# A fused attention and MLP kernel: first q load with a cast, k' and q' of the leftover chunks through one exponential, a new instruction order

## The chip, the cores and the metric

The kernel runs on one core of one Trainium2 chip. The metric is the device time of one execution in microseconds (us), as the median of several runs. The profile is that of one execution.

A core has a matmul engine (PE in the profile, its weight loads PEld), a vector engine (DVE), a scalar engine (ACT), GpSimd (POOL) and a queue engine (SP). Each works through its own list of instructions in order and waits on semaphores. Transfers are issued by SP, ACT or POOL and run on 16 shared DMA engines. In this kernel every load that changes the type is issued by POOL.

## The reference

What is computed, with the scale of the attention and the sizes put in:

```python
# q, k, v: (8, 8, 576, 64); omega: (128, 64); w_in: (512, 2048); w_out: (2048, 512)
def phi(x):                                  # x is q or k, times 64 ** -0.25
    h = einsum('bhsd,md->bhsm', x, omega) - (x * x).sum(-1, keepdims=True) / 2
    return exp(h - h.max(-1, keepdims=True)) / sqrt(128)
q_p, k_p = phi(q), phi(k)
kv  = einsum('bhsm,bhsd->bhmd', k_p, v)
num = einsum('bhsm,bhmd->bhsd', q_p, kv)
den = einsum('bhsm,bhm->bhs', q_p, k_p.sum(2)) + 1e-6
x = (num / den) as (8 * 576, 512)            # one row for each token, heads side by side
h = x @ w_in                                 # 4608 x 2048
out = (h * clip(h + 3, 0, 6) / 6) @ w_out    # 4608 x 512
```

## The kernel before

**Tiles.** The kernel goes through the 8 batches. In each batch the 8 heads are four pairs. A head has 576 positions; 512 are the "mains", 64 are the "leftovers". A batch has 36 chunks of 128 rows (`NCH`), held as 18 double chunks (`NDC`): double chunks 0 and 1 hold the leftover rows, 2 to 17 the mains. `TU` cuts the 18 into (0,2), (2,6), (6,10), (10,14), (14,18).

**Attention of a batch.** `load` (L643) brings in k, q and v; the loads of k come as mains `k00` to `k11` and leftovers `kl`, those of q as `q00` to `q11`, `ql0` and `ql1`. In batch 0 k and q arrive as float32 (`k32`, `q32`) through SP and ACT, and PE transposes them as float32 (`turns32`, L742, L748), with an evacuation from PSUM that casts to bfloat16 (the `Tev` operations, L552 on ACT, L553 on DVE). In later batches POOL issues the loads with a cast into `kb` and `qb`; batch 1 is transposed by PE in bfloat16 (`turns`, L756, L564), batches 2 to 7 by a DMA transpose (L803). The projections on omega are matmuls (batch 0: L865 for k, L884 for q; later `burst`, L808, with L822 for k and L825 for q). An exponential on ACT turns a projection in PSUM into k' (`kp`, L872 or L841) or q' (`qpT`, L888 or L849); DVE takes the row maximum of k' (`row_max`, L705). `cc` is its reciprocal; v is scaled with it (`vc` L999/L1001, `vcl` L910, `vcc` L1008/L1009); then come the products with v (`kv`, L1017/L1019), the numerators (`num`, L1045), the division (L1064/L1068) into `xb`, and its transposition into `xT` (batches 2 on: DMA, L1100) and `xS`.

**Leftovers in a burst.** A part of two double chunks, (0,2), gets two PSUM banks. One bank holds the k projection of one half of the double chunks in its first 256 columns and the q projection in its second 256. Before, each half bank has an exponential of its own, and each half of k' a row maximum: four exponentials of 256 columns and two maxima a batch, in batches 1 to 7.

**MLP.** Block b of 512 tokens is worked on while batch b + 1 goes through attention; block 8 holds all the leftover tokens. The first matmul is either plain (`mm1`, L1124: four operations of four 512-column matmuls for a group of four feature tiles) or a scheme of seven products in place of eight (`mm1_quad`, L1199: 28 matmuls of 256 columns at L1222, three PSUM copies, two additions). `FIRST7` gives for each of the four groups the first block that uses the seven products. These need sums of weights (`input_sums`, L1154, L1318) and of tokens (`x_sums`). The second matmul uses such a scheme too (`products`, L1358, L1391). The activation is a relu on ACT (L1130, L1258, L1286) and a product on DVE (L1132, L1260, L1288). Block 0 goes by halves of 256 tokens (`mm1_half`, L1265; half A first), so that it can start before the whole of x is there.

**Opening.** w_in arrives by five loads on POOL (`wi`, L625), gated by `W_GATE` on the landing of `q11`. PE runs matmuls on a constant tile (`idle_work`, L603, L606) where the plan leaves it idle in the first 21 us.

**Order.** Nothing is queued in the order of the code. Every operation has a number, by creation. The table `ORDER` gives for each of the five engines the list of operations in the order in which its queue has them; which engine runs an operation follows from the list it stands in. `schedule` (L209) goes through the lists with a plan of durations (`occ`), of times after an operation's end until others may count on it (`lat`; for batch 0's loads `LANDS`), of issue times and of shared DMA bandwidth (`packet`). From that plan come the PSUM banks, the places of the fillers and the order among engines. Semaphore waits follow from what each operation reads and writes: the kernel computes the same at any plan.

## Time and profile before

| | |
|---|---|
| runs | 299.27, 298.52, 298.09 us; median 298.52 |
| profiled execution | 298.33 us, of which the span from first to last instruction is 296.5 |
| busy: PE, PEld | 289.5 us, 220.1 us |
| busy: DVE, ACT, POOL | 257.4 us, 240.6 us, 182.2 us |
| granted PE clock | 0.999 |
| DMA | 44.90 MB, mean 151 GB/s |

A group's line gives the line of the kernel, the engine, the operation, what it writes and reads, its shape and count, then its busy time and the mean of one (ns), then the idle time of the engine just before such instructions and what ended most of it. A line of the waits gives who waited for whom, the total in us, the number of times and the longest. Matmuls are pipelined and their ends are modelled: a busy PE need not be at its peak. The numbers in `qb`, `kb` and the like are left out of names; several buffers share a name, so `q<-...` at L1318 and L1222 is the former `q32` in its second use, as a store for sums.

### The profile page before, as it was taken

Reading aid. Unit: us, or ns where it says so; the run is one execution under the profiler, and the core shown is the slowest. Engines: PE = TensorE matmul, PEld = TensorE weight load, DVE = VectorE, ACT = ScalarE, POOL = GpSimd, SP = SyncE. Lnnn points to the kernel's source line nnn. Section 1 sums busy time; section 2 is a strip of 40 time slices with the busy share of each in tenths; the row PEclk is TensorE's granted clock in tenths of the full one; section 3 lists DMA queues with packets and bytes.
Section 4 is the critical chain, followed back from the end, with each engine's and each line's share of the span. In section 5 each row is a group of like instructions: output and inputs, shape, how many; then the busy total and the mean of one; then the engine's idle time right before and its main releaser. Section 6 shows DMA issues by size and latency. Waiting matters only on the chain.

```text
span 296.5 us, 7761 instructions
## 1 busy us (share of the span) xinstructions
PE 289.5 (98%) x2938; PEld 220.1 (74%) x2938; DVE 257.4 (87%) x581; ACT 240.6 (81%) x587; POOL 182.2 (61%) x207
## 2 busy tenths in 40 slices
PE   8999999999898999999999999999999999999996
PEld 5768855544784698658856987588787888888885
DVE  4797888869987998899789996999999999998974
ACT  2975988799778998999899887999899988767410
POOL 1666456047697863898798579766667344556241
PEclk9999999999999999999999999999999999999999
DMA  8999999989999997998997999959601500110034
GB/s 234 296 206 196 203 234 117 149 200 229 138 202 207 216 127 207 152 199 234 163 180 130 111 259 168 153 131 234 122 2 35 167 25 0 74 71 2 0 144 142
DMA packets 90100, 44.90 MB, mean 151 GB/s; under 512 B 57936, under 2 KB 87760, under 8 KB 90064
## 3 DMA queue, kind: packets, MB, share of 16 engines
q1 hardware_dynamic: 62496, 31.11, 46.6%
q0 software_dynamic: 26592, 12.46, 33.9%
q10 hardware_dynamic: 976, 0.85, 0.9%
q8 instruction: 23, 0.38, 0.5%
q14 instruction: 13, 0.11, 0.1%
HBM read 36.73 MB, written 9.44 MB: 156 GB/s over the span
## 4 chain that ended last, share of the span: by engine, by line
PE 90%; ACT 6%; DVE 3%; issue 0%
PE p L1391 33%; PE p L1222 20%; PE p L1124 13%; PE p L1302 5%; PE p L1277 5%; PE p L1045 3%; PE p L822 3%; PE p L1017 3%; PE p L825 2%; ACT kp L872 1%; PE p L606 1%; ACT tsb L1130 1%; ACT qpT L849 1%; ACT qpT L888 1%; PE p L564 1%; ACT kp L841 1%
## 5 line engine op out<-in xcount | busy, mean ns | idle before, releaser
L705 DVE TENSOR_REDUCE mx<-kp 128x4 f32<-128x512 bf16 (+1 forms) x79 | 47.8, 629 | 6.1 <-ACT kp L841 4.1
L1258 ACT ACTIVATE tsb<-p 128x512 f16<-128x512 f32 x76 | 44.8, 620 | 8.0 <-DVE gT L1260 4.3
L1260 DVE SCALAR_TENSOR_TENSOR gT<-tsb,p 128x512 f16<-128x512 f16 x76 | 50.0, 679 | 1.4 <-ACT tsb L1258 1.0
L1124 PE MATMUL p<-xT,wi 128*128 128x512 f16 x208 | 49.2, 379 | 1.0 <-ACT qpT L849 0.8
L1391 PE MATMUL p<-wo,gT 128*128 128x256 f16 x368 | 46.2, 273 | 0.8 <-DVE gT L1132 0.8
L552 ACT COPY p<-p 128x512 f32<-128x512 f32 x61 | 35.3, 596 | 7.8 <-PE p L1222 5.8
L841 ACT ACTIVATE kp<-p 128x512 bf16<-128x512 f32 (+1 forms) x70 | 37.3, 578 | 4.8 <-PE p L825 4.8
L1391 PEld LDWEIGHTS p<-wo,gT 128*128 128x128 f16 x368 | 35.2, 98 | 5.3 <-ACT kp L841 1.1
L849 ACT ACTIVATE qpT<-p 128x512 bf16<-128x512 f32 (+1 forms) x70 | 37.7, 577 | 0.8 <-PE p L825 0.7
L1132 DVE SCALAR_TENSOR_TENSOR gT<-tsb,p 128x512 f16<-128x512 f16 x52 | 34.2, 678 | 4.5 <-ACT tsb L1130 4.0
L1124 PEld LDWEIGHTS p<-xT,wi 128*128 128x128 f16 x208 | 19.5, 98 | 22.4 <-ACT qpT L849 1.7
L1130 ACT ACTIVATE tsb<-p 128x512 f16<-128x512 f32 x52 | 31.4, 629 | 3.1 <-PE p L1124 2.7
L999 POOL TENSOR_TENSOR vc<-v,cc 128x512 bf16<-128x512 f32 (+1 forms) x29 | 29.1, 1002 | 7.4 <-DVE s L1318 1.9
L1318 POOL TENSOR_TENSOR gT<-gT 128x512 f16<-128x512 f16 x21 | 24.3, 1156 | 14.1 <-DVE s L1318 10.1
L1391 PE MATMUL p<-t,gT 128*128 128x256 f16 x256 | 31.1, 273 | 0.0
L1318 POOL TENSOR_TENSOR s<-gT,s 128x512 f16<-128x512 f16 x18 | 20.8, 1156 | 13.1 <-DVE s L1318 4.3
L1318 POOL TENSOR_TENSOR gT<-gT,s 128x512 f16<-128x512 f16 x18 | 20.9, 1162 | 12.3 <-PE p L1391 6.7
L1391 PEld LDWEIGHTS p<-t,gT 128*128 128x128 f16 x256 | 24.4, 98 | 5.0 <-issue 1.6
L652 POOL DMA_DIRECT2D kb<-in_k_dram x21 | 16.4, 785 | 18.9 <-DMA kT<-kb 10.9
L1318 POOL TENSOR_TENSOR s<-gT 128x512 f16<-128x512 f16 x15 | 17.4, 1158 | 10.3 <-DVE wi L1318 3.2
L1068 ACT ACTIVATE xb<-p,rec 128x64 f16<-128x64 f32 x98 | 21.9, 365 | 0.5 <-DVE rec L1057 0.5
L652 POOL DMA_DIRECT2D qb<-in_q_dram x28 | 19.7, 708 | 2.9 <-DMA wi<-in_moe_w_in_dram 2.9
(142 smaller groups left out, 640.3 us busy)
## 6 DMA issues: line engine op xcount, KB each, us to landing
v<-in_v_dram SPq DMA_DIRECT2D x14, 512.0 KB, 4.7
out_dram<-osb SPq DMA_DIRECT2D x14, 512.0 KB, 3.8
kb<-in_k_dram POOLq DMA_DIRECT2D x14, 256.0 KB, 6.2
qb<-in_q_dram POOLq DMA_DIRECT2D x14, 256.0 KB, 6.2
wo<-in_moe_w_out_dram POOLq DMA_DIRECT2D x8, 256.0 KB, 6.7
wi<-in_moe_w_in_dram POOLq DMA_DIRECT2D x3, 512.0 KB, 7.5
q<-in_q_dram SPq DMA_DIRECT2D x4, 256.0 KB, 4.5
vl<-in_v_dram SPq DMA_DIRECT2D x8, 128.0 KB, 3.8
```

What stands on the lines that cost most here:

```text
L552: return E.copy(dst(), src())
L652: lambda E: E.dma_start(dst, src), prio + 0.001 * turn_of[0], reads=gate, writes=keys,
L705: op("DVE", dvet(128 * n), lambda E: E.reduce_max(dst, src, axis=AX.X), p, reads=reads, writes=writes, name="mx" + name)
L841: op("ACT", actt(128 * (d1 - d0)), lambda E, lh=lh, ko=ko, part=part: E.activation(ko, out_of(part, 0, lh)[0].rearrange("p (x m) -> p x m" ...
L849: op("ACT", actt(128 * (d1 - d0)), lambda E, lh=lh, part=part: E.activation(qd[:, part[0]:part[1], lh, :], out_of(part, 1, lh)[0].rearrang ...
L1124: ins = E.matmul(ring.t[vh.slot], wi[:, c, 128 * f:128 * f + 128], xv[:, c, :], start=(c == 0), stop=(c == NJ - 1))
L1130: op("ACT", actt(512), lambda E: E.activation(tsb[tu][:], ring.t[vh.slot], AF.Relu, bias=0.5, scale=1.0 / 6.0), t - 0.1, reads=[vh], write ...
L1222: ins = E.matmul(bank(v)[:, 256 * g:256 * g + 256], w(c, f + g), x[:, c, :], start=start and g == 0 and c == 0, stop=c == 1, skip_group_ch ...
L1258: op("ACT", actt(512), lambda E, v=v, tu=tu: E.activation(tsb[tu][:], bank(v), AF.Relu, bias=0.5, scale=1.0 / 6.0), t - 0.1, reads=[v], wr ...
L1260: op("DVE", dvet(512), lambda E, v=v, tu=tu, dst=dst: E.scalar_tensor_tensor(dst, pieces(tsb[tu][:]), 1.0, pieces(bank(v)), ALU.min, ALU.m ...
L1318: op(engines, {"POOL": 0.157 + n / 475.0, "DVE": 0.08 + n / 2000.0}, lambda E: E.tensor_tensor(dst, x, y, ALU.subtract if minus else ALU.a ...
L1391: ins = E.matmul(ring.t[v.slot][:, 256 * j:256 * j + 256], a[:, f, 128 * j:128 * j + 128], w[:, f, :], start=(first and f == 0 and j == 0) ...
```

## The change

The q of batch 0 is loaded into `qb` with a cast, by POOL, as in the other batches; it is transposed by `turns` in bfloat16 and evacuated from a bfloat16 bank. `W_GATE` names the last main chunk of `qb` in place of `q32`. SP's list loses six loads and POOL's gets them, ahead of `wi`.

`kp` and `qpT` become the two halves of one tensor `kq`. In a burst's part of two double chunks one exponential reads a whole bank and writes 256 columns into each half. So there are two exponentials of 512 columns a batch in place of four of 256, and one row maximum in place of two.

`FIRST7` is (7, 7, 2, 2) in place of (6, 7, 2, 2): the first group of block 6 is plain, and the weight sums of groups 0 and 1 are made together, in four additions in place of eight. The weight sums no longer wait for q's transposes.

The plan's numbers change: `LANDS`, a new `LANDS_B` for the later loads, and several `lat`, those of the DMA transposes, of w_out and of the stores. All five lists of `ORDER` are rewritten; 1,963 operations are left of 1,996. In the lists of batch 0 two evacuations of q go from ACT to DVE, two of DVE's five `vc` halves to POOL, one `vcc` from POOL to ACT, and the evacuation into `xS` from DVE to ACT.

```diff
--- before.py
+++ after.py
@@ ORDER, the POOL list alone; the other four lists are rewritten as fully @@
-        1, 2, 4, 3, 36, 34, 35, 186, 187, 184, 183, 203, 37, 38, 258, 259, 257, 236, 260, 261, 268, 270, 267, 263, 269,
+        1, 2, 4, 3, 33, 23, 26, 25, 24, 32, 36, 34, 35, 186, 37, 183, 184, 187, 202, 219, 235, 38, 258, 260, 257, 261,
...
@@ -450,8 +447,9 @@
     LATE = 0.4
     FIRST = [("k", 1), ("k", 0), ("q", 1), ("v", 0), ("v", 1), ("q", 0)]
     REST = [("k", 1), ("k", 0), ("q", 1), ("q", 0), ("v", 0), ("v", 1)]
-    LANDS = {"ql0": 2.3, "ql1": 2.3, "v00": 2.1, "q01": 2.1, "v11": 1.0, "v01": 0.2, "k01": 1.8, "vl": 1.8, "q11": 1.8}
-    W_GATE = [("q32", 1, 3)] * 4
+    LANDS = {"k00": 0.9, "k10": 0.9, "kl": 1.2, "q00": 0.9, "q10": 0.9, "ql0": 1.3, "ql1": 1.3, "v00": 1.3, "v10": 1.1, "q01": 1.1, "v11": -0.8, "v01": -0.1, "k01": 1.0, "k11": 0.7, "vl": 1.1, "q11": 1.0}
+    LANDS_B = {"vl": 0.2, "v00": 0.5, "v10": 0.9, "ql0": 0.8, "ql1": 0.8, "kl": 1.1}
+    W_GATE = [("qb", 17)] * 4
     alpha = float(D) ** -0.25
     PE_T, PE_X = 2, 2
     SPARE = 1
@@ -490,8 +488,9 @@
         X4s.append(at.rearrange("p (c t) -> p c t", c=2))
     kT = sbt("kT", [128, NDC, 128], BF16)
     qT = sbt("qT", [128, NDC, 128], BF16)
-    qpT = [sbt("qpT", [128, NCH * 128], BF16)] * 2
-    kp = [sbt("kp", [128, NCH, M], BF16)] * 2
+    kq = sbt("kq", [128, 2, NCH * 128], BF16)
+    qpT = [kq[:, 1, :]] * 2
+    kp = [kq[:, 0, :].rearrange("p (c m) -> p c m", m=M)] * 2
     mx = [sbt("mx%d" % u, [128, NCH], F32) for u in range(2)]
     cc = [sbt("cc%d" % u, [128, NCH], F32) for u in range(2)]
     vc = [sbt("vc%d" % u, [128, 520], BF16) for u in range(2)]
@@ -631,9 +630,9 @@
 
     def w_out_piece(g, gate):
         f0, f1 = WO[g]
-        op("POOL", 0.7375 * (f1 - f0), lambda E: E.dma_start(
+        op("POOL", 0.66 * (f1 - f0), lambda E: E.dma_start(
             wo[:, f0:f1, :], w_out[128 * f0:128 * f1, :].rearrange("(c p) e -> p c e", p=128)),
-           -0.2 + 0.05 * g, reads=gate, writes=[("wo", g)], group="dwo%d" % g, inc=16, lat=0.9, name="wo%d" % g,
+           -0.2 + 0.05 * g, reads=gate, writes=[("wo", g)], group="dwo%d" % g, inc=16, lat=1.2, name="wo%d" % g,
            issue=0.85, packet=91.0)
 
 
@@ -646,11 +645,11 @@
         turn_of = [0]
 
         def dma(part, dst, src, n, keys, gate, prio, run):
-            cast = b > 0 and part[0] in "kq"
+            cast = b > 0 and part[0] in "kq" or part[0] == "q"
             e = "POOL" if cast else eng[turn_of[0]] if turn_of[0] < len(eng) else "SP"
-            op(e, n * (0.74 if b == 0 else 0.8) * (1.0 if run == 1024 else 1.5) / 262144.0,
+            op(e, n * (0.74 if not cast else 0.8) * (1.0 if run == 1024 else 1.5) / 262144.0,
                lambda E: E.dma_start(dst, src), prio + 0.001 * turn_of[0], reads=gate, writes=keys,
-               group="d" + part + ("c" if cast else "") + (str(pb) if b and part != "v" else ""), inc=16, lat=LANDS.get(part, 1.5) if b == 0 else 1.1,
+               group="d" + part + ("c" if cast else "") + (str(pb) if b and part != "v" else ""), inc=16, lat=LANDS.get(part, 1.5) if b == 0 else LANDS_B.get(part, 1.2),
                name="%s.%d" % (part, b), issue=(0.63 if part[1] == "l" and part[0] == "q" else 0.77) if cast else 0.62 if b else 0.53, packet=50.0 if run == 1024 else 18.0)
             turn_of[0] += 1
 
@@ -658,7 +657,7 @@
 
         def landing(t, hh, m0, m1):
 
-            if t == "v" or b == 0:
+            if t == "v" or b == 0 and t == "k":
                 return [(t + "32", hh, m) for m in range(m0, m1)]
             return [(t + "b", 2 + 4 * m + 2 * hh + x) for m in range(m0, m1) for x in range(2)]
 
@@ -680,7 +679,7 @@
             if t == "q":
                 for hh in range(2):
                     dma("ql%d" % hh, dst[64 * hh:64 * hh + 64, 0:NP, :],
-                        src[b, hh:H:2, MAIN:S].rearrange("m s d -> s m d"), 65536, [("q32l", hh)] if b == 0 else lefts_of(t, hh),
+                        src[b, hh:H:2, MAIN:S].rearrange("m s d -> s m d"), 65536, lefts_of(t, hh),
                         gates[t], base[t], 256)
             else:
                 sap = src[b].rearrange("(m h) s d -> m (h s) d", h=2)[:, MAIN:MAIN + 128, :]
@@ -688,7 +687,7 @@
                     sap.rearrange("m x d -> x m d"), 131072, [("vl", pb)] if t == "v" else [("k32l", 0)] if b == 0 else lefts_of(t, 0),
                     gates[t], base[t], 256)
 
-        tensors = {"k": (k, kb if b else k32), "q": (q, qb if b else q32), "v": (v, v32)}
+        tensors = {"k": (k, kb if b else k32), "q": (q, qb), "v": (v, v32)}
         for t, part in FIRST if b == 0 else REST:
             (mains if part else lefts)(t, *tensors[t])
 
@@ -790,9 +789,9 @@
                 for m0, m1 in HALVES:
                     nm = "%d%s" % (m0 // 2, "AB"[s])
                     dbl = every(m0, m1, s)
-                    turns32("q", nm, dbl, alts(qT, s, m0, m1), q32, main_keys("q", range(m0, m1)), 0)
-            for t, src, dst in (("k", k32, kT), ("q", q32, qT)):
-                turns32(t, "l", [0, 1], dst[:, 0:2, :], src, left_keys(t), 0 if t == "k" else LATE)
+                    turns("q", nm, dbl, alts(qT, s, m0, m1), qb, 0)
+            turns32("k", "l", [0, 1], kT[:, 0:2, :], k32, left_keys("k"), 0)
+            turns("q", "l", [0, 1], qT[:, 0:2, :], qb, LATE)
         elif b < PE_T:
             for t, src, dst in (("k", kb, kT), ("q", qb, qT)):
                 for i, (d0, d1) in enumerate(TU):
@@ -804,7 +803,7 @@
                         dst[:, x0:x1, :], flat(cst[:, 2 * x0:2 * x1, :])),
                        pos(4.5 * i) - 0.1, reads=rows_of(t, range(x0, x1)),
                        writes=[(t + "T", x) for x in range(x0, x1)], group="d%sT%d" % (t, i), inc=16,
-                       lat=1.0, name="Tdma%s.%d.%d" % (t, b, i), issue=1.42, packet=24.0)
+                       lat=0.4, name="Tdma%s.%d.%d" % (t, b, i), issue=1.42, packet=24.0)
         def burst(n, ranges):
             parts = [(d0, d1, [Virt(ring, True) for _ in range(2 if d1 - d0 == 2 else 4)]) for d0, d1 in ranges]
 
@@ -833,9 +832,20 @@
             op("PE", SWITCH + 2 * mmt(128 * total), e, p0,
                reads=[(t + "T", x) for t in "kq" for d0, d1 in ranges for x in range(d0, d1)] + omk, writes=virts,
                alloc=virts, lat=0.25, slack=sl, dslack=2 * sl, name="R%d.%d" % (b, n))
-            qd = qpT[pb][:].rearrange("m (x l t) -> m x l t", l=2, t=128)
+            qd = qpT[pb].rearrange("m (x l t) -> m x l t", l=2, t=128)
             for part in parts:
                 d0, d1, _ = part
+                if d1 - d0 == 2:
+                    for lh in range(2):
+                        op("ACT", actt(512), lambda E, lh=lh, part=part: E.activation(
+                            kq[:].rearrange("p w (x l m) -> p w x l m", l=2, m=M)[:, :, part[0]:part[1], lh, :],
+                            ring.t[part[2][lh].slot].rearrange("p (w x m) -> p w x m", w=2, m=M), AF.Exp, scale=alpha),
+                           p0, reads=[part[2][lh]], writes=[(w, 0, d, lh) for d in range(d0, d1) for w in ("kp", "qpT")],
+                           name="eK%d.%d.%d" % (b, d0, lh))
+                    both_h = [(d, lh) for d in range(d0, d1) for lh in range(2)]
+                    row_max(b, "%d.%d.0" % (b, d0), kp[pb][:, 2 * d0:2 * d1, :], mx[pb][:, 2 * d0:2 * d1], 4, p0 + 0.01,
+                            [("kp", 0) + h for h in both_h], [("mx", pb) + h for h in both_h], False)
+                    continue
                 for lh in range(2):
                     ko = kp[pb][:, 2 * d0:2 * d1, :].rearrange("p (x l) m -> p x l m", l=2)[:, :, lh, :]
                     op("ACT", actt(128 * (d1 - d0)), lambda E, lh=lh, ko=ko, part=part: E.activation(
@@ -889,7 +899,7 @@
                     dst(lh), ring.t[vQ.slot][:, 0:n].rearrange("m (j t) -> m j t", t=128), AF.Exp, scale=alpha),
                    p + 0.045 * lh, reads=[vQ], writes=[("qpT", 0, x, lh) for x in dbl], name="eQ%d.%s" % (b, name))
 
-        qv = qpT[pb][:].rearrange("m (x l t) -> m x l t", l=2, t=128)
+        qv = qpT[pb].rearrange("m (x l t) -> m x l t", l=2, t=128)
         for i, (d0, d1) in enumerate(TU):
             if b < ROWS and (i == 0 or b):
                 project(str(i), list(range(d0, d1)), qT[:, d0:d1, :],
@@ -939,7 +949,7 @@
         else:
             op("SP", 0.6, lambda E: E.dma_start_transpose(
                 xs0[pb][:], xb[pb][0:64, NJ * 512:XW]),
-               pos(12), reads=[("xb", 0, j, 2) for j in range(NJ)], writes=[("xs0", pb)], group="dxS%d" % pb, inc=16, lat=1.0,
+               pos(12), reads=[("xb", 0, j, 2) for j in range(NJ)], writes=[("xs0", pb)], group="dxS%d" % pb, inc=16, lat=0.2,
                name="Sdma.%d" % b, issue=1.33, packet=24.0)
             op(("ACT", "POOL"), {"ACT": 0.5, "POOL": 0.85}, evac(lambda: woven(b), lambda: xs0[pb][:]), pos(12) + 0.05, port="POOL",
                reads=[("xs0", pb)], writes=[("xS", b)], name="Swv.%d" % b)
@@ -1100,7 +1110,7 @@
             op("SP", 0.9, lambda E: E.dma_start_transpose(
                 xT[pb][:, m, :].rearrange("p (t k) -> p t k", t=4), xm[pb][:, m, :]),
                t + 0.03, reads=[("xb", 0, m, x) for x in range(2)], writes=[("xT", pb, m, x) for x in range(2)],
-               group="dxT%d_%d" % (pb, m), inc=16, lat=1.8, name="Xdma" + nm, issue=1.34, packet=24.0)
+               group="dxT%d_%d" % (pb, m), inc=16, lat=1.2, name="Xdma" + nm, issue=1.34, packet=24.0)
 
 
     hcount = [0]
@@ -1134,7 +1144,7 @@
            t - 0.1, reads=[vh, ("t", tu)], writes=[("gT", gu, f, x) for x in range(2)], name="g.%d.%d" % (blk, f))
 
 
-    FIRST7 = (6, 7, 2, 2)
+    FIRST7 = (7, 7, 2, 2)
     SEVEN0 = False
     XADD = ("DVE", "POOL")
     AHEAD = 2
@@ -1157,7 +1167,7 @@
         r = slice(f0, f0 + n)
         wa = [[wi[:, 2 * j:2 * j + 2, 1024 * i + f0:1024 * i + f0 + n] for j in range(2)] for i in range(2)]
         lo, hi = wik(h), wik(2 + h)
-        old = [(t + "32", hh, m) for t in "kq" for hh in range(2) for m in range(NP)] + [("k32l", 0), ("q32l", 0), ("q32l", 1)]
+        old = [("k32", hh, m) for hh in range(2) for m in range(NP)] + [("k32l", 0)]
         t = FIRST7[g0] - 0.6
         w = [["W%d%d" % (i, g) for g in range(g0, g1)] for i in range(5)]
         combine("W3", W3s[:, :, r], wa[0][0], wa[1][0], True, 2 * n, t, lo + hi, w[3] + old, ("DVE",))
@@ -1490,7 +1500,7 @@
             src = osb[:, r:r + n, c0:c1] if n > 1 else osb[:, r, c0:c1]
             op(("SP", "ACT") if blk == 8 else "SP", {"SP": occ, "ACT": occ}, lambda E, src=src, dst=dst: E.dma_start(dst, src), t,
                reads=keys if n > 1 else [k for k in keys if k[1] == r], writes=[("out", blk, i, c0, r)],
-               group="doutw%d_%d_%d" % (r, c0 if blk == 8 else 0, n), inc=16, lat=1.1, name="outw.%d.%d" % (blk, i),
+               group="doutw%d_%d_%d" % (r, c0 if blk == 8 else 0, n), inc=16, lat=0.5, name="outw.%d.%d" % (blk, i),
                issue=0.5, packet=84.0)
 
     def mlp(blk):
```

## The prediction

> **What bounds the kernel now.** I read the page's busy shares first, then the chain of waits by engine, then the busy time by stretch, then the instruction groups of the edited lines, and last the waits and landings of the opening. The page and its chain:
>
> ```profile
> span 296.5 us, 7761 instructions
> PE 289.5 (98%) x2938; PEld 220.1 (74%) x2938; DVE 257.4 (87%) x581; ACT 240.6 (81%) x587; POOL 182.2 (61%) x207
> PE 90%; ACT 6%; DVE 3%; issue 0%
> ```
>
> PE fills the span, and 90% of the chain that ends last is PE's. So an edit counts only where PE waits, where PE's own work changes, or in the opening. The stretches (columns: length; busy time of PE, PEld, DVE, ACT, POOL; clock; DMA share; GB/s) say where PE waits:
>
> ```profile
> 5.00:10.00 5.00, 5.00 (x42) 4.23 (x42) 2.18 (x4) 3.16 (x7) 1.20 (x2) 1.00 1.13 321
> 10.00:23.00 13.00, 12.34 (x148) 8.53 (x146) 12.61 (x42) 10.56 (x28) 8.57 (x14) 1.00 1.21 234
> 23.00:50.00 27.00, 27.00 (x258) 19.01 (x256) 23.13 (x50) 22.92 (x54) 14.01 (x21) 1.00 1.25 199
> 50.00:100.00 50.00, 48.05 (x480) 29.43 (x477) 42.48 (x103) 42.27 (x109) 31.93 (x37) 1.00 1.10 187
> 100.00:150.00 50.00, 49.87 (x558) 39.01 (x556) 44.64 (x103) 46.39 (x126) 37.53 (x42) 1.00 1.02 176
> 150.00:280.00 130.00, 130.00 (x1321) 105.40 (x1320) 120.58 (x256) 111.25 (x263) 83.03 (x84) 1.00 0.56 105
> ```
>
> From 23 to 280 us PE idles 1.95 + 0.13 = 2.08 us, nearly all of it between 50 and 100. From 150 on it never idles; there only PE's own work counts. Before 23 us PE looks busy, but 35 of its instructions are fillers of L606 and the rest waits for q', k' and x: there DVE (12.61 of 13) and ACT set the pace. The two large idle times in the middle are named by PE's waits between 50 and 150 us:
>
> ```profile
> PE p L1124 <- ACT qpT L849: 0.8, 1, 0.8
> PE p L1391 <- DVE gT L1132: 0.8, 1, 0.8
> ```
>
> Both stand behind the bursts that hold the leftover chunks (around 74 and 91 us). The groups of the edited instructions, by form:
>
> ```profile
> L841 ACT ACTIVATE kp<-p 128x512 bf16<-128x512 f32 x56 | 33.2, 621 | 2.0 <-PE p L825 2.0
> L849 ACT ACTIVATE qpT<-p 128x256 bf16<-128x256 f32 x14 | 5.6, 410 | 0.2 <-PE p L825 0.2
> L841 ACT ACTIVATE kp<-p 128x256 bf16<-128x256 f32 x14 | 5.4, 407 | 2.8 <-PE p L825 2.8
> L705 DVE TENSOR_REDUCE mx<-kp 128x4 f32<-128x512 bf16 x65 | 42.6, 676 | 5.3 <-ACT kp L841 3.2 <-ACT kp L872 1.9
> L705 DVE TENSOR_REDUCE mx<-kp 128x2 f32<-128x256 bf16 x14 | 5.7, 412 | 0.9 <-ACT kp L841 0.9
> ```
>
> Half the columns cost two thirds of the time, so joining two pays. Last, the loads: the wait of the weights for q, and issue to landing (us):
>
> ```profile
> POOL wi L625 <- DMA q<-in_q_dram: 6.6, 1, 6.6
> qb<-in_q_dram POOLq DMA_DIRECT2D x14, 256.0 KB, 6.2
> q<-in_q_dram SPq DMA_DIRECT2D x4, 256.0 KB, 4.5
> ```
>
> **Part 1, the opening.** Six q loads go from SP to POOL. POOL's setup ends at 2.19 us and it then waits until 8.80, so six issues of 0.63 to 0.78 us (4.4 together) fit there; `wi` is queued behind them, but waits for q11 in any case. ql1 and q00 go first, so q11 starts at 2.19 + 0.63 + 0.78 = 3.6 us (before: about 4.1) and q10 at 5.2 (before 5.1). Landing: the trace has no cast load in the empty opening. Its nearest rows are SP's q loads (4.0 to 5.2 us) and the later cast loads into qb (3.4/5.5/8.4, minimum, median, maximum). With 5.5, q11 lands at 9.1 instead of the 8.8 at which `wi` started, and q10 at 10.7; the first q transposes of before start at 10.53. On SP the v loads move up by six issues of about 0.5 us, and POOL's `vc` no longer waits for v (0.49 and 0.38 us at 11.6 and 12.6). I take the landings as a draw.
>
> [...]
>
> What the cast saves: PE's 18 f32 transposes at 0.109 us apart become bf16 ones at 0.056, −0.95 us, hidden (fillers of L606 stand between them). The order table moves two q evacuations from ACT to DVE and one `vcc` onto ACT: ACT −0.604 −0.418 +0.248 = −0.77 us (its bf16 copy takes 0.598, so no gain each). DVE gets two more (0.422 + 0.282), its third goes from 0.639 to 0.422, and two `vc` halves of 0.467 go to POOL: −0.45 us. The slower of these two engines paces the opening; I take **−0.6 us**, between the two. Bounds: −1.22 (both count), and +1.9 if q10 takes the 8.4 of the latest cast load: 5.2 + 8.4 = 13.6 is 3.0 behind 10.53, less two k' exponentials (1.1 us) that the new ACT order puts ahead of q. The next q load (batch 1, 22.6 us) now must wait for transposes that end near 13 us: no cost.
>
> **Part 2, the joined exponential.** In each of 7 batches four exponentials of 256 columns become two of 512, and two row maxima become one. No row shows one with two separated destinations; bounds are the 512 row and twice the 256 row. I take the 512 row, which has its size. ACT: 4 × 0.408 − 2 × 0.62 = 0.39 us a batch; DVE: 2 × 0.412 − 0.676 = 0.15. On the path that is only where PE waits behind such a burst, at 74 us (DVE) and 91 us (ACT): 0.39 + 0.39 gives **−0.8 us**; bounds 0 (something else is late next) and −1.6 (both waits gone). Elsewhere PE's queue covers it. New waits: the row maximum needs both exponentials, with only DVE's reciprocals behind it; the k' half waits for the previous batch's last numerators, which in the order of before lie 3.6 us or more ahead.
>
> **Part 3, block 6.** FIRST7 turns one quad of seven products into four plain `mm1`: 16 × 0.216 − 28 × 0.109 = **+0.41 us** of PE work where PE never idles. It also takes three copies and two adds from ACT and DVE (about 3.2 us) and merges eight weight sums into four (−0.6 us of DVE): worth nothing where PE is never late. Below: −0.1 if such evacuations do hold PE up.
>
> **Part 4, the new order.** Every queue is rearranged; the lat and LANDS numbers are a planner's inputs and cost nothing by themselves. By the counts of the table ACT gets 461 operations instead of 487, and by their rows some 11 us less work. Of the idle 2.08 us part 2 leaves 1.28. The part of ACT's relief that falls in the 50 us where PE idles is 11 × 50 / 296.5 = 1.9 us, more than is left, so I take all of it, **−1.28 us**. Bounds: −1.28 and +2.1 (the same idle made once more elsewhere).
>
> **Sum.** −0.6 − 0.8 + 0.41 − 1.28 = −2.27. The profiled execution took 298.33 us (span 296.5 and 1.8 around it), so 296.06; it lies 0.19 below the median 298.52, which makes 296.2 in terms of that median, 0.8% less.
>
> **Rivals.**
> - *Nothing reaches PE:* the opening ends with `wi` and x as before, the joined exponential is no shorter than its two parts (then it would not do what it says) or another engine is last at 74 and 91 us. For it: DVE is 97% busy from 10 to 23 us. Against: the 0.8 us behind ACT's qpT. Between −0.6 and +0.41: about 298.2.
> - *Landings counted too early (slower):* the new order rests on transposes through DMA that land 0.6 us sooner than assumed before (kT, qT: 1.0 to 0.4; xT: 1.8 to 1.2). PE is in order, so a burst placed ahead of its kT or qT stops everything behind it. For it: those for qT land after 3.4/4.1/8.4 us, a long tail; against: no such wait shows between 50 and 150 us. Price: 0.6 us at the first burst of each of six batches, 3.6; with parts 1 to 3, 298.33 − 1.0 + 3.6 = 300.9. It decides once such waits of PE exceed 1.6 us together.
> - *q late (slower):* 8.4 us to landing, +1.9 in place of −0.6: 298.33 + 1.9 − 0.8 + 0.41 = 299.8. It decides when q10 lands after about 11.6 us.
>
> **How the numbers follow.** A measurement of this kernel can tell about 0.5% (1.5 us) from no change: faster means below 297.0, slower above 300.0. Forecast 0.52, nothing reaches PE 0.23, late landings 0.15, q late 0.10. The forecast's own range is 294.6 to 297.6: the low end has all idle gone, both engines' savings and the hidden transposes (298.33 − 2.08 − 1.22 + 0.41 − 0.95 = 294.5), the high end half of parts 1, 2 and 4 (298.33 − 1.34 + 0.41 = 297.4, and 0.19). About 0.06 of the forecast lies above 297.0, and of q late 0.04 below 300.0. So faster 0.46, same 0.06 + 0.23 + 0.04 = 0.33, slower 0.15 + 0.06 = 0.21. The range reaches from 294.6 to 300.2: left out are most of the late landings and the ends.
>
> **What would show it.** Right: the q transposes of batch 0 start by 10.7 us and the half-A `mm1` runs unbroken 0.6 us sooner; 14 exponentials near 0.62 us with two outputs, 14 of 256 columns gone; the two 0.8 us idle times of PE at 74 and 91 us are shorter; 28 matmuls of L1222 are gone and 16 of L1124 added; PE idles under 1 us from 23 to 280 us. Wrong: PE waiting for DMA of kT, qT or xT; the first q transposes after 11.6 us; or PE idle of 2 us and more after 23 us.

## The result, and the profile after

The changed kernel took 298.64 us (median; 298.13 to 301.17) beside 298.09 us for the kernel before, measured with it: 1.0046 times the time, 95% interval 1.0029 to 1.0064. (The ratios of this document are those of the measurement and not quotients of the medians, which here are 0.55 us apart.) A second measurement gave 299.09 us and 1.0051 [1.0026, 1.0076], with medians 1.5 us apart. So by the ratio the change cost about 1.4 us (0.9 to 1.9 by the interval), at the edge of the 1.5 us that the prediction called no change, where 2.3 us less was forecast. The profiled execution took 301.17 us, at the slow end of these runs.

The page of that execution, its span, busy shares and the chain that ended last:

```profile
span 299.4 us, 7714 instructions
PE 289.9 (97%) x2930; PEld 220.0 (73%) x2930; DVE 257.9 (86%) x576; ACT 233.6 (78%) x552; POOL 187.6 (63%) x215
PE 90%; DMA 3%; ACT 2%; DVE 2%; POOL 1%; issue 1%; POOLq 0%
```

ACT has lost 7.0 us of work, where the prediction counted some 11, and PE has about as much as before (289.9 us for 289.5). But 3% of the chain, 9.6 us, is now DMA, which was not in it. The stretches (length; busy PE, PEld, DVE, ACT, POOL; clock; DMA share; GB/s) say where PE waits:

```profile
5.00:10.00 5.00, 4.98 (x46) 4.26 (x43) 2.03 (x3) 2.83 (x6) 1.39 (x3) 1.00 1.25 258
10.00:23.00 13.00, 8.99 (x81) 5.32 (x79) 8.60 (x25) 8.39 (x23) 7.17 (x12) 0.87 1.10 178
23.00:50.00 27.00, 26.96 (x295) 20.40 (x296) 24.36 (x56) 20.18 (x43) 15.82 (x24) 1.00 1.23 202
50.00:100.00 50.00, 49.81 (x489) 30.05 (x487) 44.57 (x108) 43.14 (x106) 34.14 (x40) 1.00 1.02 171
100.00:150.00 50.00, 50.00 (x548) 39.39 (x546) 45.15 (x104) 44.97 (x121) 37.45 (x42) 1.00 1.12 193
150.00:280.00 130.00, 129.00 (x1305) 103.02 (x1303) 118.96 (x251) 109.26 (x253) 84.04 (x85) 1.00 0.56 108
```

Two things stand against each other. From 50 to 100 us PE is busy for 49.81 us instead of 48.05: the gain that was forecast seems to be there (the second profile of the kernel before, b0 below, halves it). From 10 to 23 us PE is busy for 8.99 instead of 12.34 us, at a mean clock of 0.87. The waits of PE name the first cause, and that of POOL and the loads of the opening show it (load lines: count, KB each, median us from issue to landing; first v of the kernel before, then both loads of the changed one):

```profile
PE p L563 <- DMA qb<-in_q_dram: 3.3, 2, 3.0
PE p L1134 <- ACT kq L851: 1.0, 1, 1.0
```

```profile
v<-in_v_dram SPq DMA_DIRECT2D x4, 256.0 KB, 5.3
```

```profile
v<-in_v_dram SPq DMA_DIRECT2D x4, 256.0 KB, 9.4
qb<-in_q_dram POOLq DMA_DIRECT2D x4, 128.0 KB, 8.4
```

Before, q took 4.5 us from issue to landing on SP's queue and v, behind it, 5.3. Now q takes 8.4 us and the four v loads beside it 9.4. The main loads land in turn: q at 10.08, v at 11.20, q at 11.57, v at 12.72, q at 13.12, v at 14.25, q at 14.62 and v at 15.41 us. The chain of waits through the opening:

```profile
2.18 2.85 POOL qb L651 x4
5.03 9.59 DMA qb<-in_q_dram
14.62 0.05 issue
14.67 1.20 PE p L563 x12
```

The last main load of q, q10, is issued at 5.03 us (5.2 was forecast) and lands at 14.62. The first transposes of q, L563, run at 13.17 us instead of 10.53. `wi`, which waits for q11, is issued from 11.86 us on (9.1 was forecast, before it was 8.80), and the first product with w_in starts at 24.3 us instead of 18.8. Two more losses are in this run and not in the second profile of the same kernel (298.87 us): the clock,

```profile
15.00:17.50 2.50, 2.50 (x17) 1.63 (x14) 2.35 (x7) 2.45 (x5) 0.86 (x2) 0.50 1.22 189
17.50:20.00 2.50, 2.30 (x8) 0.74 (x6) 2.50 (x7) 1.54 (x5) 1.97 (x4) 0.82 1.15 173
```

which was granted at 0.50 from 15.0 to 18.4 us, after PE's wait of 3.0 us; and a wait at 153 us, to which the last experiments come back.

### The profile page after: what moved, and what is told of

Same layout as the page of the kernel before. It is cut to its first block, busy times and chain, and to the rows that moved or that the text cites. A ratio compares the mean times of both kernels' runs of the same rounds, so it can differ in the third digit from the quotient of the medians.

```text
span 299.4 us, 7714 instructions
## 1 busy us (share of the span) xinstructions
PE 289.9 (97%) x2930; PEld 220.0 (73%) x2930; DVE 257.9 (86%) x576; ACT 233.6 (78%) x552; POOL 187.6 (63%) x215
## 4 chain that ended last, share of the span: by engine, by line
PE 90%; DMA 3%; ACT 2%; DVE 2%; POOL 1%; issue 1%; POOLq 0%
PE p L1401 32%; PE p L1232 18%; PE p L1134 17%; PE p L1287 5%; PE p L1312 4%; PE p L821 3%; DMA qb<-in_q_dram 3%; PE p L1055 3%; PE p L1027 3%; PE p L824 2%; ACT kq L898 1%; PE p L563 1%; POOL qb L651 1%; DVE xb L1074 1%; PE p L894 1%; PE p L1474 1%
## 5 line engine op out<-in xcount | busy, mean ns | idle before, releaser
L1134 PE MATMUL p<-xT,wi 128*128 128x512 f16 x224 | 53.0, 380 | 1.2 <-ACT kq L851 1.0
L704 DVE TENSOR_REDUCE mx<-kq 128x4 f32<-128x512 bf16 x72 | 47.1, 674 | 7.4 <-ACT kq L882 3.1
L1268 ACT ACTIVATE tsb<-p 128x512 f16<-128x512 f32 x72 | 42.1, 613 | 10.8 <-PE p L1232 7.3
L1328 POOL TENSOR_TENSOR gT<-gT,s 128x512 f16<-128x512 f16 x23 | 26.6, 1155 | 24.7 <-PE p L1401 15.8
L1134 PEld LDWEIGHTS p<-xT,wi 128*128 128x128 f16 x224 | 20.8, 98 | 24.9 <-issue 1.9
L1009 POOL TENSOR_TENSOR vc<-v,cc 128x512 bf16<-128x512 f32 (+1 forms) x31 | 30.3, 978 | 13.2 <-PE p L1029 5.0
L551 ACT COPY p<-p 128x512 f32<-128x512 f32 x59 | 34.3, 598 | 3.3 <-PE p L1401 2.3
L859 ACT ACTIVATE kq<-p 128x512 bf16<-128x512 f32 x56 | 33.9, 626 | 1.6 <-PE p L824 1.3
L851 ACT ACTIVATE kq<-p 128x512 bf16<-128x512 f32 x56 | 32.3, 614 | 2.8 <-PE p L824 2.6
L651 POOL DMA_DIRECT2D qb<-in_q_dram x34 | 24.0, 716 | 11.2 <-DMA wo<-in_moe_w_out_dram 8.5
L1328 POOL TENSOR_TENSOR gT<-gT 128x512 f16<-128x512 f16 x17 | 19.9, 1168 | 7.9 <-DVE s L1328 3.1
L1074 DVE TENSOR_TENSOR xb<-p,rec 128x256 f16<-128x256 f32 (+1 forms) x44 | 19.8, 471 | 0.3
```

Source lines behind the costliest of these rows:

```text
L551: return E.copy(dst(), src())
L651: lambda E: E.dma_start(dst, src), prio + 0.001 * turn_of[0], reads=gate, writes=keys,
L704: op("DVE", dvet(128 * n), lambda E: E.reduce_max(dst, src, axis=AX.X), p, reads=reads, writes=writes, name="mx" + name)
L859: op("ACT", actt(128 * (d1 - d0)), lambda E, lh=lh, part=part: E.activation(qd[:, part[0]:part[1], lh, :], out_of(part, 1, lh)[0].rearrang ...
L1134: ins = E.matmul(ring.t[vh.slot], wi[:, c, 128 * f:128 * f + 128], xv[:, c, :], start=(c == 0), stop=(c == NJ - 1))
L1268: op("ACT", actt(512), lambda E, v=v, tu=tu: E.activation(tsb[tu][:], bank(v), AF.Relu, bias=0.5, scale=1.0 / 6.0), t - 0.1, reads=[v], wr ...
```

## The experiments

Three theories were stated first. **A**: q on POOL's queue and v on SP's queue share the DMA engines, so that v, which stood behind q in one queue, now takes its bandwidth. **B**: a load with a cast is slow by itself. **C**: the loss lies elsewhere, in block 6 or the new order. The table gathers what the runs below say on the opening; each number is from one profile, "first w_out" is the start of PE's first product with w_out, which closes the opening, and the ratio is that of the timed runs to those of the kernel before that were measured with them.

| kernel | q queue | v queue | q11, q10 land | last v lands | first w_out | ratio |
|---|---|---|---|---|---|---|
| before | SP | SP, behind q | 8.5, 10.0 | 14.0 | 38.0 | 1 |
| after | POOL, cast | SP | 11.6, 14.6 | 15.4 | 42.4 | 1.0046 |
| a1: after again | POOL, cast | SP | 11.6, 14.6 | 14.4 | 41.1 | 1.0051 |
| a2 | SP | SP, behind q | 8.7, 10.2 | 14.2 | 38.5 | 0.9967 |
| a3 | POOL, cast | SP, after q11 | 8.9, 10.2 | 22.0 | 43.8 | 1.0095 |
| a6 | POOL, cast | POOL, behind q | 8.1, 9.5 | 13.6 | 37.7 | 0.9938 |
| a6 again | POOL, cast | POOL, behind q | 9.0, 10.4 | 14.0 | 38.4 | 0.9941 |
| b1: before's order | POOL, cast | SP | 10.8, 13.5 | 13.2 | 40.8 | 1.0090 |
| b5: before's order | SP | POOL | 12.1, 13.6 | 12.2 | 41.1 | 1.0137 |

**The changed kernel again (a1),** with no edit. 

> The changed kernel once more, on the chip that runs the next three. Theories. A (shared transfer): batch 0's q, now on POOL's queue, moves at the same time as v on SP's, each gets about half of the DMA engines, so q11 lands at 11.6 and q10 at 14.6 us (before: 8.5 and 10.0), PE stands at the q transposes and the opening is 3 to 5 us longer; the rest of the kernel gained 1 to 2 us. B (slow cast load): q lands late because a cast load issued by POOL is slow by itself, whatever else moves. C (elsewhere): the opening is not what costs; block 6 and the new order are. All expect 298.3 to 299.0 us here; A and B expect q10's landing after 13 us in this profile too and PE idle of 2 us or more between 10 and 15 us.

Measured: 299.09 us, 1.0051 [1.0026, 1.0076]. Of its runs, five had a mean clock of 0.994 and took 299.77 to 301.47 us; the others took 297.89 to 299.32. The profiled run is one of the others (298.87 us), though PE waited 2.8 us for q in it.

**Undo the load of q alone (a2).** The six loads go back to SP as float32, with before's transposes and before's `LANDS`; everything else of the change stays.

```diff
-            cast = b > 0 and part[0] in "kq" or part[0] == "q"
+            cast = b > 0 and part[0] in "kq"
-    W_GATE = [("qb", 17)] * 4
+    W_GATE = [("q32", 1, 3)] * 4
```

> The changed kernel with batch 0's q loaded as before, by SP, as float32, with float32 transposes; all else of the change stays, its order too. A and B: q10 lands at about 10 us, no stand at the q transposes, 1.5 to 3 us faster than the changed kernel: 295.5 to 297.0. C: within 0.5 us of the changed kernel.

Measured: 296.86 us, 0.9967 [0.9951, 0.9983]. The rest of the change is a gain of 1.0 us, and the load of q turns it into a loss: C is out as the cause of the loss.

**Do the load of q alone (b1).** The kernel before, with q loaded by POOL with a cast, ahead of `wi` in POOL's list, and transposed in bfloat16; the plan has the change's `LANDS`.

```diff
-            cast = b > 0 and part[0] in "kq"
+            cast = b > 0 and part[0] in "kq" or part[0] == "q"
-    W_GATE = [("q32", 1, 3)] * 4
+    W_GATE = [("qb", 17)] * 4
```

> The kernel before with the cast load of batch 0's q alone: six loads from SP to the head of POOL's list, bfloat16 transposes; its own order otherwise. A and B: q10 lands at 13 to 15 us and it is 1.5 to 4 us slower than before: 299.5 to 302. C: within 0.7 us of before.

Measured: 300.61 us, 1.009 [1.0062, 1.0118]. The same edit costs 2.7 us in the old order too, so it is not the new order that makes it costly.

**Hold v back (a3).** The changed kernel, with the v loads of batch 0 gated on the landing of q11.

```diff
-            load(0, ("SP", "ACT", "SP", "ACT"), {t: [] for t in "kqv"})
+            load(0, ("SP", "ACT", "SP", "ACT"), {"k": [], "q": [], "v": [("qb", 17)]})
```

> The changed kernel with batch 0's v loads held back until q11 has landed; q is still a cast load by POOL. A: with v out of the way q11 lands at 8 to 9.5 us and q10 at 9.5 to 11, v lands from 12 to 17; the stand at the q transposes goes, some of it returns at the first products with v: 296.5 to 298.0. B: q11 and q10 land no more than 1 us sooner than in the changed kernel, and v later still, so 299.5 or more. C: within 0.5 us of the changed kernel.

Measured: 300.86 us, 1.0095 [1.0059, 1.013]. With v out of the way the cast load is as quick as SP's, q10 at 10.24 us: B is out. But v now moves beside the weights, takes 8.3 us from issue to landing (5.3 before), and its last load lands at 22.0 us, so the time is worse still (299.09 for a1). Part of that is the clock: five of the six runs had a mean of 0.994 (300.84 to 301.85 us, the sixth 298.63), and the profile shows 0.94 from 23 to 50 us.

**v beside q without any cast (b5).** The kernel before, with v of batch 0 issued by POOL ahead of the weights, and q where it was, on SP.

```diff
-            e = "POOL" if cast else ...
+            e = "POOL" if cast or b == 0 and part[0] == "v" else ...
```

> The kernel before, q still float32 by SP and no cast, with one thing changed: the five v loads of batch 0 are issued by POOL, ahead of the weights, instead of by SP behind q. Theory A, two queues share the DMA engines and a load loses the place it had in one queue: q is late without any cast, q11 lands at 10.3 to 11.5 us and q10 at 12.5 to 14.5 (before 8.5 and 10.0), v earlier than before, and the time goes up by 1.5 to 4 us, ratio 1.005 to 1.013. Rival, POOL's casting loads are slow: here nothing on q is cast, q lands where it did (q11 8.5 to 9, q10 10 to 10.5) and the ratio is 0.998 to 1.002.

Measured: 301.85 us, 1.0137 [1.0116, 1.0158]. No cast, and q is as late as in the change. Its loads:

```profile
v<-in_v_dram POOLq DMA_DIRECT2D x4, 256.0 KB, 6.5
q<-in_q_dram SPq DMA_DIRECT2D x4, 256.0 KB, 8.1
```

**v behind q on POOL's queue (a6).** The changed kernel with b5's one line, the five v loads in POOL's list behind the six of q, and the plan's landings of q and v set for that order.

```diff
-            e = "POOL" if cast else ...
+            e = "POOL" if cast or b == 0 and part[0] == "v" else ...
```

> The changed kernel with the five v loads of batch 0 issued by POOL, behind its six q loads, instead of by SP beside them; the loads and the cast are the same, only the queue of v differs. Theory A, two queues that share the DMA engines delay q: with k ahead on SP's queue and v behind q on POOL's, q11 lands by 9.2 us and q10 by 10.7 (before 8.5 and 10.0, changed kernel 11.6 and 14.6), v where it landed before (10.6 to 14.5), PE's wait near 10 us is under 1 us, and the ratio is 0.994 to 0.998. Rival, POOL's queue is slow in this stage by itself, or its issue of eleven loads is: q10 lands after 12 us or the last v after 17 us, and the ratio is 1.000 or more.

Measured: 295.86 us, 0.9938 [0.9917, 0.996]; once more 296.02 us, 0.9941 [0.9918, 0.9965]. Its loads and its opening:

```profile
v<-in_v_dram POOLq DMA_DIRECT2D x4, 256.0 KB, 4.1
qb<-in_q_dram POOLq DMA_DIRECT2D x4, 128.0 KB, 4.4
```

```profile
10.00:23.00 13.00, 11.82 (x144) 8.06 (x142) 11.88 (x41) 10.64 (x29) 9.61 (x15) 1.00 1.16 219
```

By the medians q now takes 4.4 us and v 4.1 (5.4 and 4.8 in the second profile). Same cast and same issuing engine for q as in the change; only that v follows in the same queue. A is shown, from both sides: v beside q makes q late without any cast (b5: q10 at 13.6 us), and with v behind it a cast load lands about as early as SP's (a6: q10 at 9.5 and 10.4 us, before 10.0; with v in the other queue 14.6). The second queue alone is not what delays: in a3 v was on SP's queue too, but issued from 8.9 us on, and q10 landed at 10.2. How the DMA engines divide their time between two queues no run here shows. This version beats both kernels.

**The place in PE's list (a4).** The changed kernel puts the first q transposes ahead of three k projections; here they stand behind them.

```diff
-        ..., 141, 144, 125, 135, 156, 150, 127, ...
+        ..., 141, 144, 135, 156, 150, 125, 127, ...
```

> The changed kernel with one number moved in PE's list: the first q transposes (those that need q11) stand behind the three k projections K0.0, K0.7 and K0.5 instead of ahead of them. Theory 'the place in PE's list costs': in the changed kernel PE stood 3.0 to 3.3 us at about 10.2 us for q11, and three k projections with their exponentials (about 0.55 us each on ACT) stood behind that wait; they now run inside it, so the opening is 1.0 to 1.8 us shorter and the ratio to the kernel before goes from 1.005 to 0.999 to 1.001. Theory 'the landings themselves cost': q10 lands at 14.6 us whatever PE does, the rest of the chain hangs on q; no more than 0.4 us is won and the ratio stays at 1.003 to 1.005.

Measured: 299.82 us, 1.0084 [1.0055, 1.0112]. PE's wait for q falls from 3.3 to 1.4 us and the first w_out product comes 1.2 us sooner than in a1 (39.9), but in its profile q10 landed at 13.3 us and not 14.6, and PE stood 1.8 us at 151 us for another reason (below). Three of the six runs had a clock of 0.994. The expected gain is not in the time; whether the place costs anything is not settled.

**Fill the wait (a5).** The changed kernel with the plan's landings of q set to the traced ones, so that matmuls on the constant tile stand in PE's wait.

```diff
-    LANDS = {..., "q00": 0.9, "q10": 0.9, "ql0": 1.3, "ql1": 1.3, ..., "q01": 1.1, ..., "q11": 1.0}
+    LANDS = {..., "q00": 3.55, "q10": 4.28, "ql0": 4.11, "ql1": 3.3, ..., "q01": 4.08, ..., "q11": 3.62}
```

> The changed kernel with the landings of batch 0's q in its plan set to those traced (q11 11.6, q10 14.6 us instead of 8.95 and 11.2), order and loads kept: the only difference is that matmuls on the constant tile fill PE's wait for q. Theory, part of the slower runs of the changed kernel comes from the granted clock, which fell to 0.5 for about 3 us after PE's wait of 3 us: no such run here, mean clock 0.999 or 1.0 in all, and the slow tail (299.3 to 301.5) goes; median 298.0 to 298.6, ratio 1.002 to 1.004. Rival, the drop comes in some runs whatever PE does: runs of clock 0.994 stay and the ratio stays at 1.005.

Measured: 299.59 us, 1.0067 [1.0051, 1.0082]. No run had a clock under 0.999, against five of twelve in a1. Runs with a mean of 0.994 came in the changed kernel, a1, a3 and a4, in whose profiles PE waits between 9 and 24 us (3.0, 2.8, 1.7 and 1.1 us at the longest), though not in all of their runs (a1's profile has a clock of 1.00; b1 has a wait of 2.1 us and no such run in six). In the profile of the changed kernel the clock of 0.50, from 15.0 to 18.4 us, began 1.8 us after the wait of 3.0 us had ended and while PE was busy; what sets it off no run here shows. But neither median nor ratio is lower than a1's: the drop goes with the slowest runs of the change (all over 299.7 us in a1), and it does not explain the loss.

**The joined exponential alone (b2), and again.** The kernel before with part 2 of the change: its tensor `kq` and its loop for parts of two double chunks. The joined exponentials stand where those of k' stood, the one maximum where the second stood.

```diff
+                if d1 - d0 == 2:
+                    for lh in range(2):
+                        op("ACT", actt(512), ... kq ..., name="eK%d.%d.%d" % (b, d0, lh))
...
+                    continue
```

> The kernel before with part 2 of the change alone: in batches 1 to 7 one exponential reads a whole bank of the leftover chunks, one row maximum in place of two, nothing else moved. Prediction's theory: the two idle times of PE of 0.8 us at 74 and 91 us shrink by 0.4 us each, 0.8 us less, ratio 0.997. Rival, nothing reaches PE: 5.6 + 5.4 us of ACT and 1 us of DVE are saved or not, the idle times stay, ratio 0.999 to 1.001. The joined exponential takes about 0.62 us if it costs what its size says, about 0.82 if the two separated destinations cost as two instructions.

Measured: 299.07 us, 1.0042 [1.0021, 1.0064], slower by 1.3 us. The profiled run was the slowest, 301.16 us. The chain of waits at 93 us, first of the kernel before, then of this one:

```profile
91.62 1.05 ACT qpT L849 x2
92.66 0.17 issue
92.83 1.24 PE p L1124 x5
```

```profile
92.78 1.05 ACT kq L859 x2
93.83 1.79 issue
95.62 1.46 PE p L1134 x6
```

Before, the view names ACT as what PE waited for, with 0.17 us unexplained behind it. In b2 ACT ended at 93.83 and PE stood on for 1.79 us. What landed 0.09 us ahead of PE's restart, both times, is the last transposed x of block 2: at 92.74 us before and at 95.53 here (4.9 and 6.8 us after its issue). The wait at 153 us of the changed kernel is of the same kind (landing 154.41, restart 154.50), and so is a4's (152.67, 152.76). So are a5's, b3's and b5's, each with the same 0.09 us. No view names the transpose; by this agreement the wait was for it, and the exponential only ended shortly before.

> The kernel before with the joined exponential alone, profiled a second time. In its first profile PE stood 1.0 us at 62 us and 2.7 us at 93 us, each ending 0.09 us after a DMA transpose had landed (kT 63.03, xT 95.53), while ACT had ended its exponentials 1.8 us before the second. Theory, the landing of these transposes sets the time there and varies from run to run: the same two places show waits that end with those landings, of other lengths (0.3 to 2.7 us), and the time differs by the sum of the differences. Rival, the joined exponential itself is slow or holds a bank: the waits have the same length and end with an exponential of ACT.

Measured: 298.63 us, 1.0047 [1.0024, 1.007]; the profiled run took 298.22. This time there is no wait at 62 or at 93 us; the one of 0.8 us near 75 stayed, put down to DVE's product. So the waits come and go, but by its ratios b2 is slower by 1.3 us. From the first product with w_out to the end of the span, less the waits at 62 and 92 to 93 us, both of its profiles take 257.9 us, the two of the kernel before 257.7 and 257.6; that product starts at 38.2 and 38.5 us for 38.0 and 37.8. Together this is 0.4 to 1.1 us; why, and what makes up the rest, stays open.

**The kernel before, a second profile (b0).** 

> The kernel before itself, for a second profile. Theory, the wait near 92 us hangs on the landing of the last transposed x of block 2: it has another length or is gone, as that landing is sooner or later (its transposes took 2.9 to 4.9 us from issue to landing in the first profile). The prediction's reading, that it hangs on ACT's exponential behind the burst of the leftover chunks: again 0.8 us, the same in every run, and ending with the exponential.

Measured: 297.69 us, 0.9997 [0.9978, 1.0016]. From 50 to 100 us:

```profile
50.00:100.00 50.00, 48.97 (x487) 30.40 (x486) 42.78 (x105) 43.03 (x110) 32.38 (x37) 1.00 1.11 189
```

48.97 us busy instead of 48.05: the wait at 92 us is gone without any edit, since the last x landed at 90.44 us. So 0.9 of the 2.08 us of idle time that the prediction worked with belonged to that one execution.

**The joined exponential undone in the best version (c1).** a6 with four exponentials and two maxima again, each beside the place of its joined one.

```diff
-                if d1 - d0 == 2:
-                    for lh in range(2):
-                        op("ACT", actt(512), ... kq ..., name="eK%d.%d.%d" % (b, d0, lh))
...
-                    continue
```

> The version with q and v both on POOL's queue, with the joined exponential undone: in batches 1 to 7 four exponentials of 256 columns and two row maxima, each beside the place of its joined one, the rest of the order kept. If the join is worth what the prediction said wherever PE is close behind (0.4 us at each of two places), this is 0.8 us slower than that version (295.9), ratio to the kernel before 0.9965. Theory that nothing hangs on these exponentials (the wait at 91 us of the kernel before ended 0.09 us after a landing of xT, the one at 74 us with a product on DVE): the same within 0.3 us, ratio 0.993 to 0.995. ACT back to back takes about 0.27 us for 256 columns and 0.48 for 512, so ACT loses about 0.1 us a batch, not 0.4.

Measured: 296.28 us, 0.9956 [0.9941, 0.9972], against 0.9938 for a6, which ran on another chip. Side by side on one chip:

> The version with q and v both on POOL's queue once more, on the same chip as the next run. Expected 0.994 of the kernel before (0.992 to 0.996) by all theories; with the next run it gives the worth of the joined exponential.

> The same with the joined exponential undone. The prediction's step (0.4 us at each of two places where PE waits) would make it 0.8 us slower than the run beside it; ACT's saving of 0.1 us a batch with nothing hanging on it 0 to 0.2 us; the first measurement 0.4.

Measured: 296.02 us for a6 and 296.61 us, 0.9965 [0.9947, 0.9983], for c1. By the ratios the join is worth 0.5 us in the first pair and 0.7 in the second, though the intervals of each pair overlap. By the profiles it is 0.4 to 0.5: from the first product with w_out on, a6 takes 255.9 us in both, c1 256.3 and 257.0, the latter with a wait of 0.5 us that ended 0.09 us after a q load of batch 1 had landed. The busy shares of the second pair, first of a6:

```profile
PE 288.9 (98%) x2926; PEld 220.1 (75%) x2926; DVE 257.9 (88%) x576; ACT 233.3 (79%) x552; POOL 191.3 (65%) x220
```

and of c1:

```profile
PE 289.3 (98%) x2926; PEld 219.7 (74%) x2926; DVE 258.4 (88%) x583; ACT 234.1 (79%) x566; POOL 191.2 (65%) x220
```

ACT gains 0.8 us over seven batches, 0.11 a batch. The timeline of c1's ACT (start, duration) shows why it is not 0.39:

```profile
72.66 0.38 ACT L842 ACTIVATE kq<-p 128x256 bf16<-128x256 f32 x1 [0.17 <-PE p L826]
72.94 0.38 ACT L850 ACTIVATE kq<-p 128x256 bf16<-128x256 f32 x1
73.20 0.39 ACT L842 ACTIVATE kq<-p 128x256 bf16<-128x256 f32 x1
73.47 0.40 ACT L850 ACTIVATE kq<-p 128x256 bf16<-128x256 f32 x1
73.73 1.12 ACT L842 ACTIVATE kq<-p 128x512 bf16<-128x512 f32 x2
```

One starts 0.27 us after the other, though each lasts 0.38 to 0.40: these exponentials overlap on ACT. One of 512 columns lasts 0.61 but starts 0.48 after its like.

**Block 6 alone (b3).** The kernel before with part 3 of the change; the plain products stand where the seven stood, the joined weight sums where those of the first group stood, and the last, in place, where that of the second did.

```diff
-    FIRST7 = (6, 7, 2, 2)
+    FIRST7 = (7, 7, 2, 2)
```

> The kernel before with part 3 of the change alone: the first group of block 6 by four plain products instead of the scheme of seven, its weight sums made together with the next group's. Prediction's theory: 28 matmuls of 256 columns at 0.109 us become 16 of 512 at 0.216, +0.41 us of PE where PE never idles, ratio 1.0014. Rival, the scheme's three copies and two additions did hold PE up: 0.1 us less than before, ratio 0.9997; or the freed DVE time helps elsewhere: ratio below 0.999.

Measured: 298.72 us, 1.0039 [1.0019, 1.0059], which is 0.6 to 1.8 us slower: a loss, and more than the 0.41 us of matmuls. Its profile counts 12 matmuls fewer, as said, and shows the same wait at 92 us as the first profile of before (PE's restart 0.09 us after a landing of x). From the first product with w_out on, less this wait, it takes 258.15 us and the kernel before 257.73 in its first profile and 257.57 in its second: 0.42 to 0.58 us more, close to the matmuls' 0.41. What makes up the rest of the 0.6 to 1.8 is open.

## Why the prediction was wrong

**The step that failed is part 1, "I take the landings as a draw".** It forecast −0.6 us for the opening; the load of q costs about 2.5 us (1.0051 against a2's 0.9967) instead. The landing was priced at 5.5 us, the median of later cast loads, with q10 at 10.7; it took 9.6 and q10 landed at 14.6. The prediction saw that "On SP the v loads move up by six issues" and took it for a help to POOL's `vc`. In fact that is what made q late: in one queue, before, q10 landed at 10.0 us and the last v at 14.0; in two, q and v landed in turn, q10 at 14.6 and the last v at 15.4, though q is needed first. The row that could have warned was shown: from 5 to 10 us the DMA engines had a busy share of 1.13 and moved 321 GB/s. With v moved up they had a share of 1.25 there and moved 258 GB/s, and q10 came 4.6 us later.

**The rival "q late"** named the right place and point: it decided at a q10 after 11.6 us, and q10 came at 14.6. Its 299.8 us lies near the 298.6 to 299.1 measured, but that is luck: it added 1.9 us for q and −0.39 for the rest, and measured are 2.5 and −1.0. Its 8.4 us came from the slowest of the later cast loads; a cast load in this place takes 5.2 us with v held back (a3) and 4.4 and 5.3 with v behind it (a6).

**Where the landings hold, part 1 has the right sign, and the size is not settled:** a6 against a2 is 0.9938 and 0.9941 to 0.9967, 0.8 to 0.9 us less where 0.6 was forecast, but the intervals overlap, the runs were on different chips, and v's queue differs too. The first w_out product comes 0.8 us sooner in one profile of a6 and 0.2 in the other. Transposes and evacuations changed together, and no run tells the two apart.

**Part 2, −0.8 us.** In the old order it is a loss (b2); in that of a6 it is a gain of 0.5 to 0.7 by the ratios, but not on the path that was forecast. The wait at 91 us was put down to ACT as the view names it; it ended with a landing of x. The one at 74 us, priced with ACT's 0.39 though its row names DVE, stayed at 0.8 us in b2; it is gone in the new order, with the join (a6) and without it (c1). And 4 × 0.408 − 2 × 0.62 sums durations that overlap: 0.39 us a batch against 0.11 on the engine. The joined one takes 0.606 us for 512 columns, as taken:

```profile
L840 ACT ACTIVATE kq<-p 128x512 bf16<-128x512 f32 x14 | 8.0, 606 | 3.2 <-PE p L824 3.2
```

**Part 3, +0.41 us:** right in sign; by b3's profile right in size too (0.42 to 0.58 us), by its ratio too small by 0.2 to 1.4 us in the old order. **Part 4** can be read only with the other two: a2 holds parts 2 to 4 together, −1.0 us where −1.67 was forecast. PE's idle time from 50 to 100 us did go, from 1.95 to 0.19 us, but 0.9 of it was the accident of one execution. Behind the opening the gain is no smaller than forecast: from the first product with w_out to the end a1, a2, a3 and a6 take 255.9 us, the kernel before 258.6 and, in its profile without the wait at 92 us, 257.6, so 1.6 to 2.6 us less. a2's −1.0 is smaller because its opening ends later, at 38.5 us for 38.0 and 37.8. How the gain divides between parts 2, 3 and 4 is not shown: the new order was not run alone. ACT's relief, which part 4 was reckoned from, is 7.0 us and not 11.

**"Landings counted too early"** was partly there: waits for a transposed x of 0.7 to 1.8 us in three profiles of the changed order (after, a4, a5) and none in a1, a2, a3 and a6. Before has them too, so they are not what the change brought.

Of the signs that were named, the first q transposes after 11.6 us told it wrong, as the text said they would; PE's idle time under 1 us after 23 us was missed by that one wait at 153 us.

## What to carry to other kernels

When a load moves to another queue, look at what stood behind it in the old one: in one queue, before, the loads of the opening landed in the order of issue (q10 at 10.0 us, the last v at 14.0), in two, after, q and v landed in turn (q10 at 14.6, the last v at 15.4), and the one needed first came 4.6 us later. Move the whole sequence (q and v here: 9.5 and 13.6 us in a6) or nothing. Before an idle time of one profile goes into a sum, profile the same kernel twice, and when the engine named as releaser had ended before the wait did, look for a DMA landing just ahead of the restart (0.09 us here).

## What the runs showed of the hardware

- In two queues q and v were late together (DMA share from 5 to 10 us: 1.13 before, 1.25 after): from issue to landing q took 4.5 us in one queue, 8.4 in two with a cast and 8.1 without (b5); v took 5.3, 9.4 and 6.5.
- The same DMA transpose of x, the last of block 2, took 4.9 and 4.2 us from issue to landing in two profiles of the kernel before and 6.8 in one of b2.
- Five of a1's twelve runs had a mean clock of 0.994; the profile of the changed kernel has the same mean and shows 3.4 us at half clock after PE's wait of 3.0 us. With filler matmuls in the wait no mean clock in six runs was under 0.999 (a5).
